# A rewritten end of a fused top-k attention and mixture-of-depths kernel, with its checks, half masks and gate transfers changed

## The chip, the cores and the metric

The kernel runs on one core of a Trainium2 chip. The metric is the device time of one execution in microseconds; the median of several runs is compared. The engines are named as in the profile: PE is the matrix engine (PEld its weight loads), DVE is VectorE, ACT is ScalarE, POOL is GpSimd, SP issues transfers.

## The reference

There are 8 batches, 8 heads, 576 tokens and a head dimension of 64. The first half is attention that keeps, for every query, the 32 highest scores:

```python
scores = scale * np.matmul(q, k.transpose(0, 1, 3, 2))
kth = np.partition(scores, -top_k, axis=-1)[..., -top_k:-top_k + 1]
scores = np.where(scores >= kth, scores, -1000000000.0)
attn = np.exp(scores - np.max(scores, axis=-1, keepdims=True))
attn = attn / (np.sum(attn, axis=-1, keepdims=True) + 1e-09)
x = np.matmul(attn, v)              # heads side by side: (8, 576, 512)
```

The second half is a mixture of depths: in each batch the 128 tokens with the highest gate score pass a two-layer network (512 to 1024 to 512), and the others are copied:

```python
scores = np.einsum('bsd,d->bs', x, w_gate)
top_idx = np.argpartition(-scores[b], 128)[:128]
ye = np.maximum(x[b, top_idx] @ w1, 0.0) @ w2
g = 1.0 / (1.0 + np.exp(-scores[b, top_idx]))
out[b, top_idx] = x[b, top_idx] + g[:, None] * ye
```

## The kernel before

**Units.** The 576 tokens of a batch are five tiles `t`: four of 128 tokens and one of 64 (`J` is 4, `NT` is 5, `R` is 64, `JP` is 512). A unit is one tile with two heads (for the last tile, two pairs of heads), 18 units a batch and 144 in all. The main loop (line 1210) goes over `n` and works on several units at a time: scores of unit n+1, the bound of n, what lies below the bound of n-1, the 32nd score of n-2, the mask of n-3, and weights times values of n-4.

**One unit.** PE multiplies queries and keys; ACT copies the scores to the tile `sc`. DVE takes the eight highest of seven parts (`cand`), and from these a bound (`bound`). ACT marks with a sign which scores lie above it (`sides`, with a count in `seen`), POOL multiplies (`y`), and DVE takes the eight highest of the rest (`next`); the last of them is the 32nd score. The mask `less` of a unit has two halves, one a head; `mask` (line 558) gives the first to ACT and the second to POOL, but in the units of `scatter_steps`, six in the loop, the second goes to DVE as a plain comparison. PE transposes scores and adds the mask times a large negative number, ACT takes the exponential (`pT`, `last`), and PE multiplies with the values (`av`); ACT copies to `xs`, and the sum of weights to `sums`. `normalise` takes a reciprocal on DVE and divides on POOL into `x`; `gates` (line 1070) makes the product with the gate weights on DVE (`prod`, `gate`).

**The mixture** of batch b (`mixture`, line 715) runs a step at a time between the units of batch b+1. Its gates go to DRAM (`row_dram`) and come back as one row in all partitions (`gate_row`). DVE counts how many gates are higher than each token's (`junk`, with the count in `rank`), a comparison with `slot` makes the selection matrix `pick`, and PE multiplies it with `parts` (place and gate, split into pieces by POOL in `split`) to find the rows. POOL fetches them by an indirect transfer (`xe`), PE runs the network (`h_ps`, `hT`, `y_ps`), and POOL adds the result to the output by another. The order is written out by hand: every engine wrapper `InOrder` (line 45) keeps program order, so all instructions show line 45, and lists such as `late` and `vector_late` say where a step is issued. `mix_at` gives the units of the steps; batch B-2, the last mixture in the loop, has earlier ones.

**Checks.** The fast way needs some conditions, or the general code in the `tc.If` at the end runs. `keep_least` (line 1189) takes per batch, on DVE, the least bound, the least 32nd score, and the least of a bit pattern (`low`). At the end `sure` collects all checks, and `unsure` is loaded into registers.

**The end.** After the loop four units of the last batch remain. `weigh_unit`, `values_unit` and `keep_unit` alternate between two sets of PSUM banks, the second taken from the scores' tile (`other_room`). The generator `closing` (line 862) does the last mixture: `spread` transposes the gates of four tiles and later of the last into `gate_row`, `count` counts (over 512 columns, then over 64 into `others`), three picks go to POOL and two to DVE, and the network follows with one product of 512 columns, one scaling `gy` and one indirect store. The remaining steps of the mixture of batch B-2 (`between`) lie in it.

Of the kernel before, what the change touches and what calls it, by code (L numbers as in the profile page):

```python
# [10 lines left out]
AF = mybir.ActivationFunctionType  # L11
# [37 lines left out]
def kernel(  # L49
# [45 lines left out]
    first_steps = ExitStack()  # L95
# [43 lines left out]
    least = const.tile([P, 3, B], FP32, name="least")  # L139
# [15 lines left out]
    others = const.tile([P, J], FP32, name="others")  # L155
# [28 lines left out]


# [372 lines left out]
    def mask(sc, next8, on=None):  # L558
# [5 lines left out]
        for i, engine in enumerate(on or (act, pool)):  # L564
            kth = next8[:, i, 7:8]
            if engine is act:
                act.activation(less[:, i, :], sc[:, i, :], AF.Relu, bias=kth, scale=-1.0)
            else:

                def is_less(engine=engine, i=i, kth=kth):  # L570
                    (engine or dve).tensor_scalar(
                        out=less[:, i, :],
                        in0=sc[:, i, :],
                        scalar1=kth,
                        scalar2=None,
                        op0=ALU.is_lt,
                    )

                if engine:
                    is_less()  # L580
                else:
                    vector_late.insert(0, is_less)
# [95 lines left out]
    def break_ties(t, gate, gate_row, rank):  # L678
# [14 lines left out]
        tok = stats.tile([P, 2], FP32, name="tok")  # L693
# [21 lines left out]
    def mixture(row0, pg, rank, exact=False):  # L715
# [20 lines left out]
        else:  # L736
            row_dram = drampool.tile([1, S], FP32, name="row_dram")
            sp.dma_start(
                out=row_dram[0, 0:JP].rearrange("(p j) -> p j", j=J), in_=gate[:, 0:J]
            )  # L740
            sp.dma_start(
                out=row_dram[0, JP:S].rearrange("(p j) -> p j", j=1),
                in_=gate[0:R, J:NT],
# [5 lines left out]
        for t in range(NT):  # L749
# [3 lines left out]
            def choose(t=t, n=n):  # L753
# [13 lines left out]
                if t == 0:  # L767
                    choose_slot(dve, t, n)
                else:
                    pool_late.append(lambda: choose_slot(pool, t, n))  # L770

            def choose_slot(engine, t, n):
                engine.tensor_scalar(
# [21 lines left out]
        found = stats.tile([P, 6], FP32, name="found")  # L795
        place = stats.tile([P, 2], FP32, name="place")
# [65 lines left out]
    def closing(b, pg, between):  # L862

        gate, rank = pg[0], ranks[:, b, :]
        gate_row = modpool.tile([P, S], FP32, name="gate_row")
        pick = modpool.tile([P, NT, CAP], BF16, name="pick")  # L870

        def spread(t0, t1):
            tr = ps_tr.tile([P, 2, J, P], FP32, name="ptr")
            n = R if t0 == J else P
            for t in range(t0, t1):
                pe.transpose(
                    tr[:, 0, t - t0, 0:n],
                    gate[0:n, t : t + 1].to_broadcast([n, P]),
                    ident[0:n, 0:n],
                )  # L880
            act.copy(
                out=gate_row[:, t0 * P : (t1 - 1) * P + n].rearrange(
                    "p (t i) -> p t i", i=n
                ),
                in_=tr[:, 0, 0 : t1 - t0, 0:n],
            )

        def count(t, among, rank):
            n = R if t == J else P
            junk = modpool.tile([P, S], FP32, name="junk", tag="scratch")  # L890
            dve.tensor_scalar(
                out=junk[0:n, among],
                in0=gate_row[0:n, among],
                scalar1=gate[0:n, t : t + 1],
                scalar2=None,
                op0=ALU.is_gt,
                op1=ALU.add,
                accum_out=rank[0:n, t : t + 1],
            )

        spread(0, J)
        yield
        for t in range(J):
            count(t, slice(0, JP), rank)
            if t == 1:
                yield
        yield
        spread(J, NT)
        split(*pg)
        for _ in range(2):  # L910
            next(between)
        for t in range(J):
            count(t, slice(JP, S), others)
        for t in range(J):
            (pool if t < 3 else dve).tensor_scalar(
                out=pick[:, t, :],
                in0=slot,
                scalar1=rank[:, t : t + 1],
                scalar2=others[:, t : t + 1],
                op0=ALU.subtract,  # L920
                op1=ALU.is_equal,
            )
        count(J, slice(0, S), rank)
        dve.tensor_scalar(
            out=pick[0:R, J, :],
            in0=slot[0:R, :],
            scalar1=rank[0:R, J:NT],
            scalar2=None,
            op0=ALU.is_equal,
        )  # L930
        ps = ps_av.tile([P, 512], FP32, name="av")[:, 0:6]
        place = stats.tile([P, 2], FP32, name="place")
        row_i = modpool.tile([P, 1], I32, name="row_i", bufs=2)
        g = modpool.tile([P, 1], FP32, name="g", bufs=2)
        multiply_places(ps, pick, pg)
        add_parts(place, ps)
        keep_rows(place, row_i, float(b * S), float((b + 1) * S - 1))
        xe = modpool.tile([P, HD], FP32, name="xe")
        fetch_rows(xe, out[0 : b + 1], row_i)
        dve.tensor_scalar_max(out=g, in0=place[:, 1:2], scalar1=-88.0)  # L940
        act.activation(g, g, AF.Exp, scale=-1.0)
        for _ in between:
            pass
        flush()
        flush_pool()
        yield
        dve.tensor_scalar_add(out=g, in0=g, scalar1=1.0)
        dve.reciprocal(out=g, in_=g)

        xeT = modpool.tile([P, NDC, CAP], FP32, name="xeT")  # L950
        ps = ps_tr.tile([P, 2, J, P], FP32, name="ptr")[:, 0, :, :]
        for dc in range(NDC):
            pe.transpose(ps[:, dc, :], xe[:, dc * P : (dc + 1) * P], ident)
        act.copy(out=xeT, in_=ps)
        yield
        hT = modpool.tile([P, NFC, CAP], FP32, name="hT")
        for f0 in range(0, NFC, 2):
            h_ps = (
                lambda: room_for_scores()[:, 0, 0, :],
                lambda: ps_av.tile([P, 512], FP32, name="av"),  # L960
                lambda: ps_misc.tile([P, 512], FP32, name="h_ps", tag="misc"),
                lambda: ps_tr.tile([P, 2, J, P], FP32, name="ptr")[:, 0, :, :].rearrange(
                    "p c i -> p (c i)"
                ),
            )[f0 // 2 % 4]()
            for i in range(2):
                multiply_h(h_ps[:, i * CAP : (i + 1) * CAP], f0 + i, xeT)
            act.activation(
                hT[:, f0 : f0 + 2, :],
                h_ps[:, 0 : 2 * CAP].rearrange("p (f i) -> p f i", f=2),  # L970
                AF.Relu,
            )
        ps = room_for_scores()[:, 0, 0, :]
        for fc in range(NFC):
            pe.matmul(
                ps, hT[:, fc, :], w2[:, fc, :], start=(fc == 0), stop=(fc == NFC - 1)
            )

        gy = modpool.tile([P, HD], FP32, name="gy")
# [563 lines left out]
```

## Time and profile before

| | us |
| --- | --- |
| median of 3 runs | 822.26 (820.8 to 823.27) |
| the profiled execution | 821.91 |
| its span, first to last instruction | 819.7 |
| VectorE busy | 782.5 |
| PE busy | 776.4 |
| ScalarE busy | 732.2 |
| GpSimd busy | 713.3 |

A busy PE is not PE at its peak, since matmuls are pipelined and their ends modelled; spans on POOL are rough. In rows of groups, the number after the bar is the busy time in us and then the mean of one in ns; the idle time before them follows, with what ended most of it. In timeline rows the first number is the start, the second the length, both in us; in brackets stands the idle time before.

### The profile page before, as it was taken

The numbers are of one execution on the slowest core, as the hardware profiler recorded it, in microseconds if no ns is written. First come the engines' busy times: TensorE is split into PE (matmuls) and PEld (weight loads), VectorE is DVE, ScalarE is ACT, GpSimd is POOL, SyncE is SP. The second block draws the span as 40 slices with busy tenths as digits, with TensorE's granted clock in tenths as the row PEclk, the third lists the DMA queues.
The fourth block names the chain that finished last, engine by engine and source line by source line (L and its number), as shares of the span: only waits on it lengthen the run. The fifth ranks groups of instructions, "written<-read, shape, count | busy, mean of one in ns | idle before, by whom it ended". The sixth has DMA issues, their size and how long they took to land. (4 is left out here: it accounts for less than half of the span.)

```text
span 819.7 us, 28408 instructions
## 1 busy us (share of the span) xinstructions
PE 776.4 (95%) x10215; PEld 597.1 (73%) x10215; DVE 782.5 (95%) x4650; ACT 732.2 (89%) x1567; POOL 713.3 (87%) x722
## 2 busy tenths in 40 slices
PE   8998888888999999999999999999999999999976
PEld 6766666666887777877787778877788777767744
DVE  7999999999999999999999999999999999999960
ACT  6999999999999999999999999999999999879830
POOL 4899999999999999899999999999989999899831
PEclk9999999999999999999999999999999999999999
DMA  7941115121151131422242221511305102101021
GB/s 163 296 84 40 41 53 100 34 53 29 60 112 41 28 92 24 104 47 43 64 83 52 53 40 60 112 34 35 74 27 113 28 15 66 23 14 16 2 72 30
DMA packets 122164, 50.38 MB, mean 61 GB/s; under 512 B 116448, under 2 KB 116448, under 8 KB 120992
## 3 DMA queue, kind: packets, MB, share of 16 engines
q1 hardware_dynamic: 118816, 43.94, 22.0%
q0 software_dynamic: 1728, 4.20, 2.8%
q8 instruction: 82, 1.34, 0.8%
q14 instruction: 66, 0.54, 0.3%
q10 hardware_dynamic: 1472, 0.36, 0.2%
HBM read 36.93 MB, written 11.55 MB: 59 GB/s over the span
## 5 line engine op out<-in xcount | busy, mean ns | idle before, releaser
L45 POOL TENSOR_TENSOR y<-sc,sides 128x576 f32<-128x576 f32 x288 | 365.7, 1291 | 52.4 <-ACT sides L45 49.3
L45 DVE MAX8 cand<-sc 128x8 f32<-128x82 f32 (+1 forms) x2016 | 314.0, 227 | 2.7 <-ACT sc L45 2.6
L45 POOL TENSOR_SCALAR less<-sc,next 128x576 bf16<-128x576 f32 x135 | 233.0, 1726 | 13.3 <-DVE next L45 9.7
L45 ACT ACTIVATE sides<-sc,bound 128x576 bf16<-128x576 f32 x288 | 223.0, 787 | 0.0
L45 PE MATMUL ptr<-out_of_reach,less 128*128 128x128 bf16 x1136 | 204.3, 219 | 18.5 <-POOL less L45 18.1
L45 PE MATMUL ptr<-ident,sc 128*128 128x128 f32 x1136 | 215.7, 281 | 0.0
L45 DVE MAX8 next<-y 128x8 f32<-128x584 f32 x288 | 204.4, 751 | 1.4 <-POOL y L45 1.4
L45 PEld LDWEIGHTS av<-v,pT 128*64 128x64 f32 x4544 | 144.1, 137 | 67.7 <-ACT last L45 64.7
L45 PEld LDWEIGHTS ptr<-ident,sc 128*128 128x128 f32 x1136 | 160.7, 141 | 28.1 <-issue 16.7
L45 ACT ACTIVATE pT<-ptr 128x1024 f32<-128x1024 f32 x142 | 145.3, 1023 | 32.1 <-PE ptr L45 30.1
L45 PE MATMUL ps<-kT,qT 64*128 64x288 f32 (+1 forms) x1248 | 173.9, 425 | 0.0
L45 PE MATMUL av<-v,pT 128*64 128x65 f32 x4544 | 163.7, 224 | 10.1 <-ACT last L45 9.2
L45 PEld LDWEIGHTS <-less 128*128 128x128 bf16 x1296 | 135.7, 105 | 38.0 <-POOL less L45 24.0
L45 ACT COPY sc<-ps 128x1152 f32<-128x1152 f32 x140 | 158.3, 1131 | 0.0
L45 ACT ACTIVATE less<-sc,next 128x576 bf16<-128x576 f32 x143 | 111.2, 778 | 13.2 <-DVE next L45 11.6
L45 PEld LDWEIGHTS ps<-kT,qT 64*128 64x128 f32 (+1 forms) x1248 | 95.8, 175 | 34.5 <-issue 20.8
L45 DVE MATCH_REPLACE8 cand<-best,cand 128x21 f32<-128x21 f32 (+1 forms) x576 | 98.9, 180 | 0.0
L45 DVE MAX8 best<-cand 128x8 f32<-128x21 f32 (+1 forms) x576 | 90.3, 189 | 0.0
L45 PE MATMUL h_ps<-xeT,w 128*128 128x128 f32 x464 | 65.8, 286 | 0.0
L45 PEld LDWEIGHTS h_ps<-xeT,w 128*128 128x128 f32 x464 | 55.8, 191 | 9.2 <-issue 5.8
L45 PE MATMUL y_ps<-w,hT 128*128 128x512 f32 x112 | 60.6, 636 | 0.0
L45 ACT ACTIVATION_READ_ACCUMULATOR sides<-sc,bound 128x1 f32 x288 | 60.0, 208 | 0.0
(157 smaller groups left out, 889.5 us busy)
## 6 DMA issues: line engine op xcount, KB each, us to landing
v<-in_v_dram SPq DMA_DIRECT2D x64, 128.0 KB, 3.5
out_dram<-x SPq DMA_DIRECT2D x8, 1024.0 KB
rows<-in_k_dram SPq DMA_DIRECT2D x56, 128.0 KB, 3.0
rows<-in_q_dram SPq DMA_DIRECT2D x56, 128.0 KB, 3.1
w<-in_moe_w_dram SPq DMA_DIRECT2D x2, 2048.0 KB
gate_row<-row_dram SPq DMA_DIRECT2D x7, 288.0 KB, 4.3
last<-in_q_dram SPq DMA_DIRECT2D x8, 128.0 KB
vpair<-in_v_dram SPq DMA_DIRECT2D x16, 64.0 KB, 3.9
```

Source lines behind the costliest of these rows:

```text
L45: return lambda *a, **kw: self._tc.keep_in_program_order(fn(*a, **kw))
```

## The change

In the loop:
- The check of the bounds' bits leaves `keep_least`: ACT copies each batch's bounds into a tile `bounded`, and `low` and two reductions are done once, at the end.
- DVE's half mask and the first slot of `pick` become a comparison whose results are also added up (`compare`); the sum of the mask is not used.
- The gates go to DRAM as 64 pieces of 16 bytes and 64 of 20, before as 128 of 16 and 64 of 4. The order in the row changes, which the counts don't depend on.

At the end:
- `closing` is gone, its steps stand in line. The last units use PSUM banks of their own (`ps_end`), and all their half masks are `compare` on DVE (`mask_both`).
- The gates of three tiles are spread and counted early, then the fourth's, then the last tile's. The last tile is divided on DVE. The picks are two on POOL, one on ACT in three steps, two on DVE.
- The fetched rows are transposed into two banks and copied by ACT and DVE. The checks follow, and their product on PE comes after the first layer. The second layer's product, the scaling and the store are done in two halves of 256 columns; `unsure` is loaded before the stores.

```diff
+    def compare(out, in0, scalar, op, total=None):
+        if total is None:
+            total = stats.tile([P, 1], FP32, name="some")[0 : out.shape[0], :]
+        dve.tensor_scalar(
+            out=out, in0=in0, scalar1=scalar, scalar2=None,
+            op0=op, op1=ALU.add, accum_out=total,
+        )
...
                 def is_less(engine=engine, i=i, kth=kth):
-                    (engine or dve).tensor_scalar(
+                    if engine is None:
+                        compare(less[:, i, :], sc[:, i, :], kth, ALU.is_lt)
+                        return
+                    engine.tensor_scalar(
...
             sp.dma_start(
-                out=row_dram[0, 0:JP].rearrange("(p j) -> p j", j=J), in_=gate[:, 0:J]
+                out=row_dram[0, R * NT : S].rearrange("(p j) -> p j", j=J),
+                in_=gate[R:P, 0:J],
             )
             sp.dma_start(
-                out=row_dram[0, JP:S].rearrange("(p j) -> p j", j=1),
-                in_=gate[0:R, J:NT],
+                out=row_dram[0, 0 : R * NT].rearrange("(p j) -> p j", j=NT),
+                in_=gate[0:R, 0:NT],
             )
...
                 if t == 0:
-                    choose_slot(dve, t, n)
+                    compare(pick[:, t, :], slot, rank[:, t : t + 1], ALU.is_equal)
...
     def keep_least(b, bound, kth):
-        low = stats.tile([P, per_batch, 2], I32, name="low", bufs=1)
-        dve.tensor_scalar(out=low, ...)
-        for w, of in enumerate((bound, kth, low)):
-            dve.tensor_reduce(out=least[:, w, b : b + 1], in_=of, ...)
+        at = 2 * per_batch * b
+        late.append(
+            lambda: act.copy(
+                out=bounded[:, at : at + 2 * per_batch].rearrange("p (n i) -> p n i", i=2),
+                in_=bound,
+            )
+        )
+        dve.tensor_reduce(out=least[:, b : b + 1], in_=kth, ...)
...
+    what_is_below(N - 1)
     weigh_unit(N - 4)
+    rows_ps = bank(ps_end, "av3")
+    turn_gates(0, J - 1, rows_ps)
     weighed[N - 4][2]()
-    what_is_below(N - 1)
-    mask_of(N - 3, (dve, dve))
+    keep_gates(0, J - 1, rows_ps)
+    mask_both(N - 3)
...
     weigh_unit(N - 1)
+    for t in range(2):
+        count(t, slice(0, (J - 1) * P), rank)
     gates(B - 1, J - 1)
+    count(2, slice(0, (J - 1) * P), rank)
...
+    count(J - 1, slice(0, JP), rank)
+    rden = stats.tile([P, H], FP32, name="rden")
+    dve.reciprocal(out=rden[0:R, :], in_=sums[0:R, (B - 1) * NT + J, :])
+    dve.tensor_tensor(x[0:R, J, :], xs[0:R, :, 0:D], rden[0:R, :], ALU.mult)
     store_last(last_out, x)
     gates(B - 1, J)
+    turn_gates(J, NT, tr)
+    keep_gates(J, NT, tr)
...
+    split(*pg)
+    count(J, slice(0, JP), rank)
+    for t in range(J - 1):
+        count(t, slice((J - 1) * P, S), others)
+    count(J - 1, slice(JP, S), others)
+    count(J, slice(JP, S), others)
+    for t in (0, 1):
+        pool.tensor_scalar(out=pick[:, t, :], in0=slot, ...)
+    act.activation(whole, others[:, 2:3], AF.Identity, bias=rank[:, 2:3])
+    act.activation(far, slot, AF.Abs, bias=whole, scale=-1.0)
+    act.activation(pick[:, 2, :], far, AF.Relu, bias=1.0, scale=-1.0)
+    for t in (J - 1, J):
+        dve.tensor_scalar(out=pick[0:n, t, :], in0=slot[0:n, :], ...)
...
+    for copy, half, dc in zip((act.copy, dve.tensor_copy), halves, (0, 2)):
+        copy(out=xeT[:, dc : dc + 2, :], in_=half[:, 0 : 2 * CAP])
...
+    for i in range(2):
+        for fc in range(NFC):
+            pe.matmul(halves[i][:, 0:W], hT[:, fc, :], w2[:, fc, i * W : (i + 1) * W], ...)
+    is_unsure = nc.values_load(unsure[0:1, 0:1])
+    for i in range(2):
+        dve.scalar_tensor_tensor(out=gy, in0=halves[i][:, 0:W], scalar=g[:, 0:1], ...)
+        put_rows(gy, half_i[:, i : i + 1], half_rows)
```

## The prediction

> **What bounds the kernel now.** I read the page's busy rows first, then the stages, then VectorE's waits, then the groups by shape.
>
> ```profile
> PE 776.4 (95%) x10215; PEld 597.1 (73%) x10215; DVE 782.5 (95%) x4650; ACT 732.2 (89%) x1567; POOL 713.3 (87%) x722
> ```
>
> Four engines are near full, so the shares do not name the bound. The windows by stage do (columns: stage, its length, then the busy time of PE, PEld, DVE, ACT, POOL, each with its instructions, then PE clock, DMA share, GB/s):
>
> ```profile
> 298.50:395.00 96.50, 95.02 (x1261) 73.57 (x1261) 96.39 (x577) 91.55 (x197) 88.60 (x88) 1.00 0.26 60
> 395.00:491.80 96.80, 95.04 (x1261) 73.60 (x1261) 96.14 (x578) 91.81 (x198) 88.85 (x88) 1.00 0.27 59
> 772.90:794.70 21.80, 17.23 (x230) 12.27 (x228) 14.22 (x41) 10.57 (x26) 9.94 (x16) 1.00 0.15 55
> 794.70:819.70 25.00, 17.98 (x93) 11.56 (x91) 4.70 (x26) 2.82 (x7) 3.70 (x3) 0.96 0.17 35
> ```
>
> In the loop (one batch is some 96.5 us) VectorE idles 0.1 to 0.7 us per batch: there its time is the kernel's time. From 772.9 us on nobody is full: the last 47 us are a chain of single steps. The waits of VectorE between 100 and 772 us confirm the first half, with one real stall:
>
> ```profile
> DVE junk L45 <- DMA gate_row<-row_dram: 1.8, 1, 1.8
> DVE cand L45 <- DVE best L45: 0.5, 1, 0.5
> ```
>
> So I cost the loop on VectorE alone and the end step by step. The groups of VectorE by shape give prices:
>
> ```profile
> L45 DVE CUSTOM_DVE_ANT_0 prod<-x,wg 128x512 f32<-128x512 f32 x32 | 30.3, 947 | 1.5 <-POOL x L45 1.4
> L45 DVE TENSOR_SCALAR_CACHE_REDUCE junk<-gate_row,gate 128x576 f32<-128x576 f32 x28 | 22.1, 788 | 1.9 <-DMA gate_row<-row_dram 1.8
> L45 DVE TENSOR_SCALAR low<-bound 128x36 int32<-128x36 int32 x8 | 6.9, 857 | 0.0
> L45 DVE TENSOR_SCALAR less<-sc,next 128x576 bf16<-128x576 f32 x10 | 6.6, 672 | 0.2
> ```
>
> The odd one is `low`: 36 numbers cost 857 ns on average. Its view gives 173 ns at least, 1,062 at the median; the timeline shows one at 395.09 for 1.06 us, while POOL's pair of `y` products ran from 393.58 to 396.06.
>
> **The loop, part by part.**
>
> *Bits checked at the end.* Per batch, `keep_least` loses `low` and two of three reductions. From the start of `low` to the next `cand` the timelines give 0.45, 1.52, 1.34, 1.34, 1.34, 1.33 and 1.29 us for seven batches: 8.6 in all. What stays is one reduction, about 0.13 from start to start: 0.9. So -7.7 us on VectorE. ScalarE gets a 36-wide copy per batch; the nearest row is its 128x8 `sums`, 0.22 us. I take nothing for it, because its own waits in the loop (17.6 us for `ptr` between 202 and 684 us) take it in; with that cover gone it is 7 x 0.2 = 1.4. Below nothing it cannot go, since it only adds work.
>
> Here a rule is weighed. The Trainium skill, "SBUF — State Buffer", on the shared port pair: VectorE in a two-port mode and GpSimd exclude each other for a whole instruction. That explains `low` at 1.06 against 0.17. It would also have every two-port mask blocked by POOL, so that the comparison with a sum, which I take to be out of that mode, pays. The rows say otherwise in the loop:
>
> *The half mask.* Six of the ten `less` lie in the loop, each in the unit in which POOL issues the scatter, and take 501 to 508 ns; the next instruction starts 0.42 us after (386.20 to 386.62). The four in the end take 1.52, 0.51, 1.15 and 0.52, two of them blocked. The comparison with a sum is the form of `junk`: 576 wide 788 ns, 0.80 to 0.86 from start to start with its accumulator read. So in the loop +0.41 x 6 = +2.5 us. By the rule alone, each blocked like the 1.15 row, it would be about -0.2 x 6 = -1.2. I take the rows.
>
> *The first slot.* Seven `pick` of 128 take 0.29 to 0.69 us, 1.9 us from start to start in all. With a sum, 128 wide lies between the 64-wide `junk` (0.32 apart) and the 512-wide (0.79): 0.39 x 7 = 2.7. So +0.8 us.
>
> *Gates to DRAM.* The issues and their landings:
>
> ```profile
> row_dram<-gate SPq DMA_DIRECT2D x7, 2.0 KB, 2.4
> row_dram<-gate SPq DMA_DIRECT2D x7, 0.2 KB, 7.2
> ```
>
> The first is 128 pieces of 16 bytes, the second 64 of 4 bytes, three times as long from issue to landing. SP waits 41.1 us in six batches for them; the gate row goes out only then (issued 710.37, landed after 4.3). Only batch 6, whose mixture starts early, shows it on VectorE, the 1.8 us above. "DMA: Bandwidth & Descriptors", Specifications, has every transfer under 512 B do read-modify-write; by that 20 and 16 bytes are as bad as 4, and the gain is nothing. The rows separate 16 from 4 sharply. Pieces of 20 are no row, but nearer to 16: I take a landing of 2.4 to 4 us. The stall needs 1.85 less than 7.2 to vanish, so it vanishes: -1.85; kept end 0. In the other six batches the row lands before it is asked for (131.49 + 4.3 against 139.2), so nothing. The loads queued behind on SP go out earlier, with room anyway.
>
> Loop: -7.7 + 2.5 + 0.8 - 1.85 = -6.25. PE is close behind (its weight loads wait 41.1 us for ScalarE's `last` in the five batches from 202 to 684, some 0.5 a unit, in heavy mixture units nothing), and POOL with a `divide` needs 5.5 us a unit; I let 0.5 be given back: -5.75.
>
> **The end, step by step** (clock of the profile before; DVE steps from start to start).
>
> ```profile
> 779.59 0.77 ACT L45 ACTIVATE less<-sc,next 128x576 bf16<-128x576 f32 x1 [0.95 <-DVE next L45]
> 780.33 0.52 DVE L45 TENSOR_SCALAR less<-sc,next 128x576 bf16<-128x576 f32 x1
> 781.66 0.33 PE L45 MATMUL ps<-ident,sc 128*128 128x128 f32 x1 [1.32 <-ACT xs L45]
> 787.75 1.04 POOL L45 TENSOR_TENSOR x<-xs,rden 64x512 f32<-64x512 f32 x1 [4.54 <-DVE rden L45]
> 791.25 2.40 POOL L45 TENSOR_SCALAR pick<-slot,ranks,others 128x128 bf16<-128x128 f32 x3
> 798.31 0.63 PE L45 MATMUL ptr<-ident,xe 128*128 128x128 f32 x4 [0.66 <-DMA xe<-out_dram,row_i]
> 806.86 7.03 PE L45 MATMUL ps<-w,hT 128*128 128x512 f32 x16
> 814.01 0.75 DVE L45 SCALAR_TENSOR_TENSOR gy<-ps,g,xe 128x512 f32<-128x512 f32 x1 [14.77 <-PEq L1506]
> 815.04 1.01 POOL L45 DMA_INDIRECT out_dram<-gy,row_i  x1 [14.44 <-DVEq L1506]
> ```
>
> - Masks: all six halves on VectorE, 6 x 0.86 + 3 x 1.33 for `next` from 771.51: done at 780.7. Before, with two on ScalarE but two blocked, 780.85. Even. `sides` of the last unit go ahead of an exponential, so POOL's `y`, 778.76 before, is there at about 777 and not waited for.
> - The last transposes: before, PE waited until 781.66 for the bank that `xs` was copied from. Separate banks leave only the mask: they end at 781.75 instead of 783.3. Values and copies follow; `sums` at 785.5 instead of 787.45.
> - VectorE no longer has four 512-wide counts before the last tile (three tiles' columns are spread early and counted 384 wide). Divide on VectorE, 64x512, the length of the 0.69 `prod`, instead of POOL's 1.04: gate of the last tile ready at 787.35 instead of 789.9, -2.55.
> - Counts of the rest: 192 wide 0.45 x 3, 64 wide 0.32 x 2, behind the 0.78 count of the last tile that covers PE's and ScalarE's turn: done 790.2. Picks: two on POOL (0.61 to 0.80 each, behind `split`, done 790.2), one on ScalarE in three steps of about 0.3 (790.4), two on VectorE (790.95). PE is through at 791.2 instead of 794.0: -2.8.
> - Place, row, fetch, landing unchanged, 4.2 us: rows at 795.4. The 3.7 us of y products in between still fit (791.2 to 794.9).
> - Transposes and copy in halves on ScalarE and VectorE: 1.15 instead of 1.37 from landing to first product: -0.2. The checks (now 288 wide, about 5 us) run on VectorE under the 7.2 us of h products; their one product costs PE 0.15.
> - Output in two halves: the second scaling is 128x256, 0.45 instead of 0.75: -0.3. Both halves take PE 3.5 us each, the same 7.03.
>
> Together -2.8 - 0.2 + 0.15 - 0.3 = -3.15; a smaller last transfer may give 0.2 more. I take -3.3.
>
> **Sum.** -5.75 - 3.3 = -9.05 against 821.91 of the profiled execution (span 819.7, 2.2 around it), which lies 0.35 under the median of the runs, 822.26. Against the median: 813.2.
>
> **Rivals.**
> 1. *Pieces of 20 bytes land as late as those of 4.* For it: only 16 is measured fast; against: 4-byte pieces are four times as many to each 16. The 1.85 stays: 815.1. Chance 0.21.
> 2. *The loop gives back.* PE, ScalarE or POOL, all at 92 to 98% of a batch, end the unit in which `low` was taken out; half of the 4.4 (the loop without the stall) returns, 2.2 instead of my 0.5: 814.9. For it: PE's waits are nothing in some mixture units; against: 0.5 a unit elsewhere, and five score tiles of depth. Chance 0.17.
> 3. *The second half's scatter waits.* It is ordered behind the landing of the first, since both write the output: first issued about 808.0, landed 3.1 later as the last one does now, 811.1; the second is ready at 811.5. Only 0.4 of room; if the first takes 5.0 like the accumulating scatters, +1.5: 814.7. Chance 0.05.
> 4. *Slower: the dot products meet POOL.* `prod` takes 0.67 free, 1.94 at worst, 947 ns at the mean of 32. The shift of VectorE against POOL can raise that. All is lost when the mean of 40 rises by 9.05 / 40 = 0.23, to 1.18 us; slower by over 0.3% beyond 1.24: 825. Against: POOL's order hangs on VectorE's results each unit, so phases come back. Chance 0.09, of which 0.05 ends within 0.3% of before.
>
> That the change does not take effect is no case: the order of instructions has every step.
>
> **Numbers.** Main case 0.48: 813.2, its own range 811 to 815 (collisions of `prod`, up to 12 us in all now, may also fall). Rivals 1 to 3 end at 814.7 to 815.1, 1 and 2 together at 816.8, with part of 3 at 817.5. Below, a third of the collisions gone: 809. About 0.3% (2.5 us) is what a measurement here tells from no change. Faster 0.91, same 0.05, slower 0.04.
>
> **What would show it.** Right: no `low` in the loop; `junk` without a DMA wait; both `row_dram` issues near 2.4 to 4 us; loop `less` at 0.79; the last batch's fetch about 2.8 us nearer to the end of the loop; from landing of rows to end some 20.9 instead of 21.4. Wrong: `prod` above 1.1, new waits of `cand` or `next` on ScalarE or POOL in the loop, a POOL wait ahead of the last scatter.

## The result, and the profile after

The changed kernel takes 817.04 us (815.27 to 817.24, six runs) where the kernel before took 821.72 beside it: a ratio of 0.9936, with an interval of 0.9921 to 0.995. It is faster by 4.7 us, about half of the 9.05 forecast. It lies outside the main case's own range of 811 to 815 us and within the 809 to 817.5 us over which the prediction spread all its cases.

The page's busy row:

```profile
PE 777.2 (95%) x10231; PEld 600.3 (74%) x10231; DVE 784.2 (96%) x4655; ACT 730.3 (90%) x1577; POOL 721.8 (89%) x722
```

Four engines are still near full, and VectorE is as busy as before although work was taken from it. In the profiled execution (817.24, span 815.4) a first load landed later, so that the first `next` starts at 20.86 us instead of 18.96. The change has no part in that; a later run of the same kernel starts at 18.81, and two of the six executions here took 815.3 and 815.4 us. Loops are therefore compared below from their own first `next`.

The windows by stage, two batches of the loop and the two parts of the end, in the columns of the prediction (busy time of PE, PEld, DVE, ACT, POOL, then PE clock, DMA share, GB/s):

```profile
303.71:399.64 95.93, 94.87 (x1264) 73.42 (x1262) 95.78 (x576) 91.15 (x198) 90.48 (x88) 1.00 0.26 60
399.64:495.57 95.93, 94.86 (x1264) 73.40 (x1263) 95.79 (x576) 91.18 (x198) 90.50 (x88) 1.00 0.26 60
770.40:791.20 20.80, 18.95 (x245) 13.87 (x244) 17.34 (x55) 11.32 (x30) 9.47 (x15) 1.00 0.15 58
791.20:815.40 24.20, 17.77 (x108) 14.48 (x106) 5.86 (x27) 2.75 (x7) 4.18 (x4) 0.93 0.17 37
```

A batch now takes 95.93 us instead of 96.5 to 96.8, the end 45.0 us from the `next` of unit 141 on instead of 48.15.

The groups that answer to those of before (busy us, then the mean in ns):

```profile
L45 DVE CUSTOM_DVE_ANT_0 prod<-x,wg 128x512 f32<-128x512 f32 x32 | 34.6, 1082 | 0.4 <-POOL x L45 0.3
L45 DVE TENSOR_SCALAR_CACHE_REDUCE less<-sc,next 128x576 bf16<-128x576 f32 x12 | 9.3, 797 | 0.0
L45 DVE TENSOR_SCALAR_CACHE_REDUCE junk<-gate_row,gate 128x576 f32<-128x576 f32 x28 | 22.1, 788 | 0.0
```

`junk` has no wait for a DMA any more, `less` costs 797 ns, and `prod` has become 135 ns longer at the mean. The issues of the gates land in 2.0 us (16-byte pieces) and 1.6 us (20-byte pieces), where the 4-byte pieces took 7.2:

```profile
row_dram<-gate SPq DMA_DIRECT2D x7, 1.0 KB, 2.0
row_dram<-gate SPq DMA_DIRECT2D x7, 1.2 KB, 1.6
```

Unit by unit the loop shows two things. At `keep_least` VectorE gains 1.02 to 1.25 us in six batches and 0.2 in the first, 6.8 in all. In the very next unit it loses 0.19 to 0.78 again, 4.0 in all, because the `prod` there has become longer. The timeline at one of these places, first of before, then of after (start, length):

```profile
398.95 2.53 POOL L45 TENSOR_TENSOR y<-sc,sides 128x576 f32<-128x576 f32 x2
401.62 1.73 POOL L45 TENSOR_SCALAR less<-sc,next 128x576 bf16<-128x576 f32 x1
402.26 0.67 DVE L45 CUSTOM_DVE_ANT_0 prod<-x,wg 128x512 f32<-128x512 f32 x1
```

```profile
400.37 2.53 POOL L45 TENSOR_TENSOR y<-sc,sides 128x576 f32<-128x576 f32 x2
402.00 1.45 DVE L45 CUSTOM_DVE_ANT_0 prod<-x,wg 128x512 f32<-128x512 f32 x1
402.86 0.67 POOL L45 TENSOR_TENSOR y<-steps,seen 128x16 f32<-128x16 f32 x1
```

Before, `prod` came 0.8 us after POOL's two passes of `y`; now it comes into the second pass, waits for its end at about 402.9, and then holds up POOL's next step in turn. The trace books the wait as VectorE's busy time, so no view of waits shows it. This is what the prediction's fourth rival described. The experiments ask whether it is the cause of the loss or only its form.

The end stands nearly as it was forecast:

```profile
785.28 0.68 DVE L45 CUSTOM_DVE_ANT_0 prod<-x,wg 64x512 f32<-64x512 f32 x1
787.41 1.58 POOL L45 TENSOR_SCALAR pick<-slot,ranks,others 128x128 bf16<-128x128 f32 x2
788.78 0.59 DVE L45 TENSOR_SCALAR pick<-slot,ranks,others 128x128 bf16<-128x128 f32 x2
789.74 0.31 PE L45 MATMUL av<-parts,pick 128*128 128x6 bf16 x3 [0.51 <-ACT pick L45]
794.31 0.66 PE L45 MATMUL av<-ident,xe 128*128 128x128 f32 x4 [0.63 <-DMA xe<-out_dram,row_i]
802.55 0.19 PE L45 MATMUL av<-ones,sure 128*1 128x1 f32 x2
810.64 0.96 POOL L45 DMA_INDIRECT out_dram<-gy,half_i  x1 [2.44 <-POOLq L1578]
```

The last tile's gate, the picks and the places come one after the other without a long wait; ScalarE's `pick` is the last of the five; the check's product runs behind the first layer; the last store waits for nothing but its branch.

### The profile page after: what moved, and what is told of

It reads as the page before. It is cut to its first block, busy times and chain, and to the rows that moved or that the text cites. A ratio compares the mean times of both kernels' runs of the same rounds, so it can differ in the third digit from the quotient of the medians.

```text
span 815.4 us, 28453 instructions
## 1 busy us (share of the span) xinstructions
PE 777.2 (95%) x10231; PEld 600.3 (74%) x10231; DVE 784.2 (96%) x4655; ACT 730.3 (90%) x1577; POOL 721.8 (89%) x722
## 5 line engine op out<-in xcount | busy, mean ns | idle before, releaser
L45 PEld LDWEIGHTS av<-v,pT 128*64 128x64 f32 x4608 | 146.1, 137 | 66.1 <-ACT last L45 62.8
L45 PE MATMUL av<-v,pT 128*64 128x65 f32 x4608 | 166.0, 224 | 8.3 <-ACT last L45 7.6
```

The costliest lines, as they stand in the source:

```text
L45: return lambda *a, **kw: self._tc.keep_in_program_order(fn(*a, **kw))
```

## The experiments

Ratios are to the kernel before, which ran beside each kernel.

### The parts alone

Four kernels are the kernel before with one part of the change. The first moves the bits to the end and leaves the old end in place (some small tiles have fewer buffers, for room):

```diff
-        low = stats.tile([P, per_batch, 2], I32, name="low", bufs=1)
-        dve.tensor_scalar(out=low, in0=bound.bitcast(I32), ...)
-        for w, of in enumerate((bound, kth, low)):
-            dve.tensor_reduce(out=least[:, w, b : b + 1], in_=of, ...)
+        late.append(lambda: act.copy(out=bounded[...], in_=bound))
+        dve.tensor_reduce(out=least[:, b : b + 1], in_=kth, ...)
...
+    flush()
+    low = modpool.tile([P, S], I32, name="low", tag="scratch")[:, 0:NS]
+    dve.tensor_scalar(out=low, in0=bounded.bitcast(I32), ...)
```

> The kernel before with only the bounds' bits moved to the end (low and two reductions leave keep_least; a copy on ScalarE; the end as before, but for 288-wide checks). Theory A (the dot product of the next unit meets GpSimd and gives it back): in batches 2 to 6 the unit of keep_least is 1.0 to 1.25 us shorter, the prod that follows takes about 1.4 us instead of 0.67, and the net is 0.3 us a batch: 2 to 3 us below before. Theory B (VectorE's saving is kept unless another engine ends the unit): prod stays at 0.67, 1.1 us a batch kept, 6.5 to 7.5 us below before.

It took 824.94 us (ratio 1.0049, interval 1.0032 to 1.0066): slower. Its loop is shorter by 2.6 us up to unit 141, which is what theory A summed up to, but not by its working: the `prod` behind `keep_least` took 1.02 to 1.05 us in five of the batches instead of 1.4, and the rest was lost at the plain masks and picks, which now waited (the masks took 1.22 us at the median). From the last unit's `next` to the end it takes 47.45 us instead of 40.87. Its timeline there:

```profile
798.00 0.31 DVE L45 TENSOR_SCALAR low<-bounded 128x288 int32<-128x288 int32 x1 [3.96 <-ACT bounded L45]
802.71 0.19 PE L45 MATMUL av<-ones,sure 128*1 128x1 f32 x2 [4.43 <-DVE g L45]
802.83 3.78 PE L45 MATMUL ps<-xeT,w 128*128 128x128 f32 x16
806.40 3.21 PE L45 MATMUL av<-xeT,w 128*128 128x128 f32 x16
```

The last copy of the bounds stands behind `gy` on ScalarE, VectorE's checks start after it and take 4.7 us, and PE has their product ahead of the first layer. Then the first layer's products take 3.78 and 3.21 us, at a granted clock of 0.50 and 0.59; in the changed kernel they take 2.05 and 1.95 at 1.00.

The second sends the gates in pieces of 16 and 20 bytes:

```diff
-                out=row_dram[0, 0:JP].rearrange("(p j) -> p j", j=J), in_=gate[:, 0:J]
+                out=row_dram[0, R * NT : S].rearrange("(p j) -> p j", j=J),
+                in_=gate[R:P, 0:J],
...
-                out=row_dram[0, JP:S].rearrange("(p j) -> p j", j=1),
-                in_=gate[0:R, J:NT],
+                out=row_dram[0, 0 : R * NT].rearrange("(p j) -> p j", j=NT),
+                in_=gate[0:R, 0:NT],
```

> The kernel before with only the gates' pieces of 16 and 20 bytes. Theory A and B alike: both transfers land after about 2 us, the one wait of the counts for the gate row (1.8 us, batch 6) is gone, and units before and after keep their lengths: 1.8 us below before. If other engines were near their bound in that unit, part of it returns: under 1 us.

819.85 us, ratio 0.9991 (0.9983 to 0.9999). The stall of the gate row is gone (1.95 us earlier in that unit), and 0.77 of it returns six units later, where a `prod` goes from 0.67 to 1.44 us.

The third writes VectorE's masks and the first slot as comparisons with a sum (here too some small tiles have fewer buffers):

```diff
-                    (engine or dve).tensor_scalar(
+                    if engine is None:
+                        compare(less[:, i, :], sc[:, i, :], kth, ALU.is_lt)
+                        return
+                    engine.tensor_scalar(
...
-                    choose_slot(dve, t, n)
+                    compare(pick[:, t, :], slot, rank[:, t : t + 1], ALU.is_equal)
```

> The kernel before with only VectorE's half mask and the first slot in the loop as comparisons with a sum (the end's masks stay plain). Theory A (a plain comparison is shorter and was not blocked in these six units): less 0.50 to 0.79 us, 0.3 us longer in each of six units and up to 0.2 in seven for the slot where it was not blocked: 1.5 to 2.5 us above before. Theory C (the plain form holds GpSimd up by as much): no change within 0.5 us, or below.

821.52 us, ratio 1.0013 (1.0002 to 1.0023): each of the six masks costs 0.3 us more (0.72 from its start to that of the next instruction, before 0.42).

The fourth has the new end, with the old loop (`closing` gone, its steps in line as in the diff of the change).

> The kernel before with only the end rewritten (checks of the bits per batch as before, plain half mask, slot and pieces in the loop as before). From the trace of the changed kernel, the end is 3.2 us shorter counted from the last unit's first steps; that should stand alone: 3.0 to 3.5 us below before. If the end gained only because the loop left the engines in another phase: under 2 us. The four parts together, if they add: the difference of the changed kernel to before, plus or minus 1 us.

817.22 us, ratio 0.9954 (0.9938 to 0.9969): 3.1 us faster, as the end was costed.

The four differences are +4.7, -0.4, +1.2 and -3.1 us, +2.4 together, while the change as a whole gives -4.9 in the repeat below. So the parts act on each other. One candidate is the end: the bits there may only pay with the check's product behind the first layer. Without the 6.6 us by which the first kernel's end was longer, the four would come to -4.2.

### The masks, the phase and the place of `prod`

The next four start from the changed kernel. First the changed kernel again:

> The changed kernel as it is, on the chip of the other three, to compare them with: 817.0 us (815 to 817.5), and in each batch but the first one dot product `prod` of about 1.45 us where the trace of before has 0.67.

815.85 us, ratio 0.9945 (0.9933 to 0.9957). `prod` has the same lengths as in the first trace of it, 0.78, 0.86, 0.97, 1.46 and 0.96 us for the five of the fifth batch.

Then the plain comparisons in the loop again:

```diff
-                    if engine is None:
-                        compare(less[:, i, :], sc[:, i, :], kth, ALU.is_lt)
-                        return
-                    engine.tensor_scalar(
+                    (engine or dve).tensor_scalar(
...
-                    compare(pick[:, t, :], slot, rank[:, t : t + 1], ALU.is_equal)
+                    dve.tensor_scalar(out=pick[0:n, t, :], in0=slot[0:n, :], ...)
```

> The changed kernel with VectorE's half masks and the first slot in the loop written as plain comparisons again (the end keeps its sums). A plain comparison of 576 numbers took 0.50 us on VectorE in the trace of before, the one with a sum 0.79. If the plain form only costs its own time, six masks become shorter by 0.3 us and the kernel is 1.8 us faster than the changed one. If the plain form waits for POOL's `y` once the loop runs earlier, as ten of them did when the bits alone were moved (median 1.22 us there), each becomes longer by 0.4 us or so, and the kernel is 2 us or more slower.

815.64 us, ratio 0.9945 (0.9932 to 0.9957): no difference, which neither expectation had. The groups say why:

```profile
L45 DVE TENSOR_SCALAR less<-sc,next 128x576 bf16<-128x576 f32 x6 | 6.6, 1097 | 0.0
L45 DVE CUSTOM_DVE_ANT_0 prod<-x,wg 128x512 f32<-128x512 f32 x32 | 29.2, 913 | 0.4 <-POOL x L45 0.3
```

The plain masks do wait now (1,097 ns at the mean; five of the six about 1.21 us, one 0.50). But `prod` becomes shorter: all forty take 37.6 us instead of 43.7 in the repeat. What is waited at one place isn't waited at the next.

The filler at `keep_least`:

```diff
-        dve.tensor_reduce(out=least[:, b : b + 1], in_=kth, ...)
+        for _ in range(4):
+            dve.tensor_reduce(out=least[:, b : b + 1], in_=kth, ...)
+        if b < B - 1:
+            spare = stats.tile([P, 8], FP32, name="spare", bufs=1)
+            dve.max(out=spare, in_=scs[per_batch * (b + 1) - 1][:, 0, :])
```

> The changed kernel with a filler at keep_least that does nothing for the result: three more small reductions of the same 36 numbers and one MAX8 over 576 scores, together about 1.07 us of VectorE's time in each batch, about what the change took away there; none of it is of a form that waits for POOL in the traces. Theory 1: what the change gained at keep_least was taken back because VectorE now reaches `prod` in the unit after it while POOL is still in `y`. Then the filler restores the old phase, `prod` there is 0.67 us again instead of 1.45, and the kernel is slower by only 0.3 us a batch, 2 us in all (819). Theory 2: VectorE's time simply adds up and the loss of 4 us lies elsewhere: then slower by 7 to 8.5 us (824 to 825.5). Theory 3: another engine ends the unit, and the filler costs nothing (817).

819.79 us, ratio 0.9988 (0.9979 to 0.9997). The filler is larger than I had worked out: 1.42 us at each place. In the next unit 0.76 to 1.06 of it comes back in the later batches, and the fourth `prod` of a batch is 0.67 to 0.68 us again. Up to the last unit 3.8 us remain of about 10. So the first theory's mechanism is there, at twice the 2 us that it put; the second, a plain sum, falls, and so does the third, no cost. From the third batch on a batch takes 96.73 to 96.75 us, and here VectorE's share is the largest:

```profile
401.56:498.30 96.74, 94.94 (x1265) 73.40 (x1261) 96.50 (x581) 91.79 (x198) 88.59 (x88) 1.00 0.25 59
```

`prod` ahead of the first head's maxima:

```diff
-            vector_late.append(lambda a=gating: gates(*a))
...
+        if gating is not None:
+            gates(*gating)
         if is_unit(n):
             bound_of(n)
```

> The changed kernel with one thing moved: the dot product `prod` and the read of its sum stand ahead of the seven `cand` maxima of the unit's first head instead of behind them, about 1.0 us earlier on VectorE. In the trace of the changed kernel a `prod` that starts while POOL is in a pass of `y` takes what is left of that pass and 0.55 us: 0.24 left gave 0.79, 0.42 gave 0.97, 0.88 gave 1.43. At the new place 0.01 to 0.24 us of a pass are left for four of the five in a batch and 0.66 for the fifth. Theory 1 (the wait for POOL's pass is what VectorE pays): 0.2 us less for each of some 35, so 3 to 7 us faster than the changed kernel (810 to 814), less where POOL's second pass, now held up by 0.55 us, comes late for somebody. Theory 3 (another engine ends the unit): no difference.

821.51 us, ratio 1.0006 (0.9998 to 1.0013), 5.7 us slower than the changed kernel beside it. Both expectations fall. The group shows that the waits grew:

```profile
L45 DVE CUSTOM_DVE_ANT_0 prod<-x,wg 128x512 f32<-128x512 f32 x32 | 36.8, 1151 | 1.4 <-POOL x L45 1.3
```

I had worked out new waits from the phase of an old trace. But the phase moved along: the five of a batch (the fifth) met 0.2 to 1.2 us of a pass in the new trace, and took 0.78, 1.24, 0.98, 1.73 and 1.04 us.

### A later place, and the port taken out

`prod` behind the maxima of both heads:

```diff
-            vector_late.append(lambda a=gating: gates(*a))
+            after_cand.append(lambda a=gating: gates(*a))
...
+        while after_cand:
+            after_cand.pop(0)()
         parts = cand.rearrange("p i (u e) -> p i u e", u=PARTS)
```

> The changed kernel with the dot product `prod` and the read of its sum moved behind the `cand` maxima of both heads, about 1.07 us later on VectorE than now. In the trace of before, a `prod` that starts after the second pass of `y` ends 1.44 us after that pass at the earliest and takes 0.67 us where it is the later; from the changed kernel's trace the five of a batch would then start 0.82, 0.75, 0.65, 0.17 and 0.65 us behind the pass and take 0.67, 0.69, 0.79, 1.27 and 0.79 us, 4.2 us together instead of 5.0. If VectorE pays each wait in full, and POOL is not disturbed because it isn't in `y`: 0.8 us a batch, 4 to 6.5 us faster than the changed kernel (809.5 to 812). If what VectorE saves at one place it waits at the next for POOL's port, so that the two engines hold each other's pace: within 1.5 us of the changed kernel.

813.77 us (813.45 to 814.21), ratio 0.9912 (0.9899 to 0.9926): faster than both kernels, the interval wholly below that of the changed kernel's repeat. At 2.1 us below that repeat it meets neither of the two ranges. The gain stops early:

```profile
300.41:395.45 95.04, 93.97 (x1255) 72.57 (x1253) 94.90 (x576) 90.28 (x195) 89.53 (x87) 1.00 0.26 61
395.45:491.38 95.93, 94.86 (x1264) 73.41 (x1263) 95.79 (x577) 91.17 (x198) 90.52 (x88) 1.00 0.26 60
```

Up to 395 us its batches are shorter than the changed kernel's but for one; from there on a batch takes the same 95.9 us, and the five `prod` again take 0.76, 0.86, 0.96, 1.43 and 0.96 us, though they stand at another place in the order.

So far the later batches end at 95.9 us or above, whether `prod` is slowed or quickened. The next two kernels ask for the floor under it. `prod` is replaced by the sum of `x` alone, in the form with a sum; the gate's weights are left out:

```diff
-        dve.tensor_tensor_reduce(
-            out=prod[0:n, 0:HD], in0=x, in1=wg[0:n, :],
-            scale=1.0, scalar=0.0, op0=ALU.mult, op1=ALU.add, accum_out=g,
-        )
+        dve.tensor_scalar(
+            out=prod[0:n, 0:HD], in0=x, scalar1=1.0, scalar2=None,
+            op0=ALU.mult, op1=ALU.add, accum_out=g,
+        )
```

> The kernel before with each dot product replaced by the sum of `x` alone in one pass (TENSOR_SCALAR_CACHE_REDUCE with 512 numbers; the gate's weights are left out, so the gates have other values): by the row of 788 ns for 576 numbers, 0.71 us or so, a form that didn't wait for POOL in any trace. The 40 dot products took 39.0 us there, so 10 us less VectorE time in it; the end has five of them. Serves as the base of the next run. If VectorE pays waits in full: 9 to 11 us faster than before; if it waits elsewhere instead: 0 to 5.

> The changed kernel with the same replacement (the gate's weights left out). Nothing of VectorE's in the loop is then of a form that waited for POOL, the 40 products' 43.7 us become 28 to 30. Theory 1 (the change's gain in the loop was eaten by `prod` waiting for POOL's `y`): the gain of the change comes out in full, this run is 8 to 10 us faster than the run with the same replacement in the kernel before, instead of 4.9. Theory 3 (the other engines set the loop's pace, and VectorE would wait for one of them): the difference stays at 5 us or falls, and VectorE shows new waits in the loop, for POOL's `y` or ACT's `sc`.

With these gates both kernels go on into the general code behind the `tc.If` (4,365 and 4,362 us), so their totals say nothing and only the loops are read. From the first `next` to that of the eighth batch the two take 662.6 and 660.3 us; with `prod` it was 669.8 and 666.9 (the latter in the repeat). The change is worth 2.3 us here and 2.9 there. The first theory's 8 to 10 us fall; the third's pace set by another engine stands. The windows of the changed kernel without `prod`:

```profile
203.96:298.30 94.34, 93.23 (x1247) 71.86 (x1246) 94.10 (x576) 89.61 (x195) 86.68 (x87) 1.00 0.27 61
393.64:489.55 95.91, 94.81 (x1269) 73.37 (x1267) 94.81 (x576) 91.16 (x199) 88.29 (x88) 1.00 0.27 60
489.55:585.48 95.93, 94.81 (x1268) 73.39 (x1265) 94.79 (x575) 91.15 (x199) 88.25 (x88) 1.00 0.25 60
```

At first VectorE runs ahead. Then a batch takes 95.9 us again, with VectorE's busy time down to 94.8, a microsecond below the length of the batch. PE's column hasn't moved: 94.81 here, 94.87 in the changed kernel.

### PE, and the check's product

The last kernel adds a small product on PE in each unit, and in the end puts the check's product ahead of the first layer:

```diff
             tr, av = room_to_turn()
+            pe.matmul(tr[:, 0, 0, :], out_of_reach, out_of_reach)
...
+    ps = bank(ps_av, "av")
+    pe.matmul(ps[0:1, 0:1], sure, ones)
+    dve.tensor_scalar(out=unsure, in0=ps[0:1, 0:1], ...)
     hT = modpool.tile([P, NFC, CAP], FP32, name="hT")
...
-    ps = bank(ps_av, "av")
-    pe.matmul(ps[0:1, 0:1], sure, ones)
-    dve.tensor_scalar(out=unsure, in0=ps[0:1, 0:1], ...)
```

> Two edits to the changed kernel that lie in different stretches of it, so that the trace tells them apart. In the loop: one more 128x128 bf16 matmul in each unit (into a tile that is overwritten at once; a row of twenty such in the trace took 1.29 us, so 65 ns each, 1.2 us in a batch of 18 units). If PE sets the pace of the later batches (95.9 us each in the changed kernel from the third on), they become longer by the whole 1.2 us or a little more, and the last unit's `next` comes 5 to 9 us later. If VectorE sets it, PE has the time to spare and nothing moves by more than 1 us. In the end: the matmul of the check (`ones`, `sure`) and the copy of its result stand ahead of the first layer again, as in the kernel before. From the last unit's `next` to the end of the span the changed kernel takes 39.4 us. If the bits at the end only pay because that matmul was moved behind the first layer, PE waits for VectorE's checks ahead of it, and the stretch takes 5 to 7 us more; if VectorE's checks would be ready anyway, less than 1 us more. Total by the first pair of theories and this: 827 to 832.

827.82 us, ratio 1.0094 (1.008 to 1.0107). The loop, two of its windows:

```profile
206.26:302.47 96.21, 95.07 (x1273) 73.33 (x1271) 95.98 (x576) 90.41 (x198) 89.69 (x87) 1.00 0.25 60
399.45:496.53 97.08, 96.03 (x1284) 74.12 (x1282) 96.94 (x576) 91.27 (x198) 90.57 (x88) 1.00 0.24 59
```

The later batches take 96.98 to 97.08 us, longer by 1.0 to 1.2 with one exception (0.8, against a 96.19 of the repeat), and PE's busy time rises by 0.8 to 1.3. The last unit's `next` comes 5.6 us later. ScalarE's 91.3 and POOL's 90.6 of 97.08 us leave room. So PE, with its own waits, sets the pace there: 94.8 us of work and about 1.0 us a batch in which its values wait for ScalarE's `last`. The row is from three batches of the repeat (total, times, longest):

```profile
PE av L45 <- ACT last L45: 3.1, 6, 0.8
```

VectorE's column rises along (96.94) although VectorE was given nothing: what it shows beyond its work is waiting for POOL inside `prod`, whose sum goes from 43.7 to 47.9 us.

In the end, from the last `next` on, it takes 46.5 us instead of 39.4: 7.1 more. PE's waits have the row, and the windows around it the clock:

```profile
PE av L45 <- DVE ones L45: 5.1, 1, 5.1
```

```profile
799.00:804.20 5.20, 0.09 (x2) 0.03 (x2) 4.71 (x23) 0.41 (x2) 1.62 (x1) 0.89 0.39 50
804.30:807.80 3.50, 3.50 (x18) 3.50 (x17) 0.14 (x1) 0.00 (x0) 0.00 (x0) 0.50 0.01 2
807.90:810.60 2.70, 2.70 (x17) 2.70 (x17) 0.00 (x0) 0.38 (x1) 0.00 (x0) 0.63 0.00 0
```

PE waits 5.1 us for VectorE's checks, and after that its granted clock is 0.50 and then 0.63 at the mean, so that the products behind it are slow as well. In the first experiment the same wait was 4.43 us and the clock behind it 0.50, and its end was longer by 6.6 us: this is what made it slower.

The lengths of the batches on VectorE, from the first `next` of one to that of the following, in us (worked out from the timelines):

| kernel | 2nd | 3rd | 4th | 5th | 6th | 7th |
| --- | --- | --- | --- | --- | --- | --- |
| before | 97.15 | 96.09 | 96.54 | 96.68 | 96.13 | 96.06 |
| changed | 96.12 | 95.48 | 95.93 | 95.93 | 95.94 | 95.91 |
| changed, filler on VectorE | 96.17 | 96.74 | 96.73 | 96.74 | 96.74 | 96.75 |
| changed, `prod` behind both heads | 95.34 | 95.63 | 95.04 | 95.93 | 95.95 | 95.90 |
| before, sum instead of `prod` | 94.06 | 95.87 | 95.88 | 95.87 | 96.01 | 95.82 |
| changed, sum instead of `prod` | 93.62 | 94.34 | 95.34 | 95.91 | 95.93 | 95.85 |
| changed, product added on PE | 96.11 | 96.21 | 96.98 | 97.08 | 96.99 | 97.01 |

The same on PE, from its first transposition of scores into `av` in one batch to that in the following. The last three columns say how far that transposition lies behind the `next` of the same unit, at the start of a batch:

| kernel | PE's 3rd | 4th | 5th | 6th | behind `next`, 3rd | 4th | 5th |
| --- | --- | --- | --- | --- | --- | --- | --- |
| before | 96.10 | 96.54 | 96.67 | 96.13 | 4.44 | 4.45 | 4.44 |
| changed | 95.90 | 95.95 | 95.90 | 95.94 | 5.82 | 6.25 | 6.26 |
| changed, filler on VectorE | 96.45 | 96.73 | 96.73 | 96.74 | 4.40 | 4.10 | 4.10 |
| changed, `prod` behind both heads | 95.90 | 95.95 | 95.91 | 95.95 | 6.11 | 6.38 | 7.28 |
| changed, sum instead of `prod` | 95.90 | 95.95 | 95.91 | 95.94 | 5.99 | 7.55 | 8.16 |
| changed, product added on PE | 96.96 | 97.12 | 96.96 | 97.01 | 5.88 | 6.62 | 6.76 |

In the kernel before, and with the filler, PE keeps a near-fixed distance behind `next` and takes VectorE's lengths: there VectorE leads, as the prediction had it, and so the filler costs time. In the changed kernel PE takes 95.90 to 95.95 us from the third batch on, also with `prod` moved behind both heads or replaced, whatever VectorE does meanwhile. VectorE's shorter batches are a lead over PE: the distance grows as long as they last (from 5.99 to 8.16 us without `prod`) and then stands. With the product added, PE's own batches take 96.96 us and more from the third on.

## Why the prediction was right, and where its size was off

The direction and the end were forecast by the right mechanism. The loop's gain was not: it was costed at 5.75 us and came to 1.4 to 3.0, by the traces compared. The total stays within the spread of the cases because the end held and because the prediction had priced a loop that gives back.

**The end: right.** Forecast -3.3, measured -3.15 from unit 141's `next` on (45.0 us instead of 48.15), and -3.1 for the end alone. Counted from that `next`, the last tile's gate comes 2.9 us earlier (forecast 2.55), the places 2.9 (2.8), the rows at the forecast time. ScalarE's pick was the last, not VectorE's. That the checks run under the first layer was costed at 0.15; their place is worth 7.1 us, which the last experiment shows.

**Bits out of the loop: right at its place, given back after it.** `keep_least` lost 6.8 us (forecast 7.7). The step that failed is "I let 0.5 be given back". The loop up to unit 141 was to gain 5.75 and gained 3.0 in the first trace and 2.3 in the repeat, each from its own first `next`. (The run with the end alone keeps the old loop, and there it took 751.7 us where the trace of before has 752.55; against it the gain is 2.1 and 1.4.) The prices of the single steps were not at fault: where they act, -6.8 for the bits, +1.8 for the masks, nothing for the slot and -1.9 for the stall are -6.9, the forecast sum -6.25. The step rests on an earlier one, that in the loop VectorE's time is the kernel's time. That holds only down to PE's pace. The second to seventh batch took 578.65 us before; six times 95.9 are 575.4, so 3.2 us were to be had there by PE's pace (and a little more as a lead), and the changed kernel took 575.31. The row for it stood in the prediction: PE busy 95.02 of 96.50 us. What I read as slack were the waits of PE's weight loads for `last` (41.1 us in five batches); of the matmuls themselves, the view of waits of before has only this between 200 and 680 us, five batches:

```profile
PE av L45 <- ACT last L45: 5.6, 12, 0.8
```

That is 1.1 us a batch, and 95.0 and 1.1 leave 0.4 of 96.5.

**How VectorE loses what it gained.** By waiting inside `prod` for POOL (sum of the forty 39.0 before, 43.0 after). In the changed kernel's trace, `prod` takes what is left of the pass of `y` that it meets and 0.55 us: 0.24 left gave 0.79, 0.42 gave 0.97, 0.88 gave 1.43. This agrees with the Trainium skill, "SBUF — State Buffer", Who interferes with whom: an instruction of VectorE with two inputs in SBUF contends with a GpSimd instruction that reads there, and the one that comes second waits for the whole of the other. Beside POOL's mask `less` the trace does not bear out the whole: the `prod` of before at 402.26 takes its free 0.67 us although `less`, which reads `sc`, runs from 401.62 to 403.35 (spans on POOL are rough). The loss looks like that contention but isn't caused by it alone: with the contention out, the later batches take the same 95.9 us. That the first batches can run below 95.9 is VectorE's growing lead over PE, as the second table shows. How PE's pace then reaches VectorE (by ScalarE's `sc` and `sides` and POOL's `y`, I suppose) was argued and not traced.

**Masks with a sum: forecast +2.5, in the changed kernel nothing.** Alone they cost 0.3 us each (costed at 0.41). In the changed loop the plain form waits (1.21 us), as the rule says that the prediction put aside, and the total is the same either way. The free rows of before (0.50 us) held for before's phase only. **The slot**, forecast +0.8, costs nothing: 347 ns, before 362 with one blocked among them.

**Gates to DRAM: right.** 1.6 and 2.0 us to land, better than the 2.4 to 4 forecast, and the stall is gone (-1.88 in that unit). Rival 1 falls. Alone, the pieces bring 0.4 us (interval of the ratio 0.9983 to 0.9999), part of the stall being waited by a `prod` again.

**The other rivals.** Rival 2, the loop gives back because another engine ends the unit, is what happened, with PE as the engine, and it came out dearer than its price of 2.2: of the 6.25 summed up, 3.3 to 4.0 were given back (up to 4.8 against the loop of the run with the end alone). The total's nearness to 816.8, the end of rivals 1 and 2 together, is luck: rival 1 did not come. Rival 3 falls: the second store waited only for its branch. Rival 4 had the right instruction and a mean of 1.08 us instead of 0.947, far from the 1.18 from which it would have eaten all.

Sum in the repeat, by span against the profile of before: 2.3 from the loop, 3.15 from the end and 0.15 from the start are the 5.6 us between 819.7 and 814.1. Between the medians it is 4.9: the traced execution of before, at 821.91 us, lies above the 820.79 of the kernel before beside the repeat.

## What to carry to other kernels

Before costing an edit on the engine that looks fullest, add up for each of the others its work and the waits of its own stream in the same stretch: the gain ends where the next of them is full, here 0.5 us a batch below. An engine's busy time can hold waiting for a port; replace the suspected instruction by one that doesn't use the port, and look whether the length of the stretch changes. And don't work out the new place of an instruction from the phases of an old trace, since the phases move along: of the two places tried, one cost 5.7 us and one brought 2.

## What was not expected of the hardware

PE's granted clock fell to 0.50 after a wait of 5.1 us, and a group of sixteen products took 3.78 us instead of 2.05; after a wait of 4.43 us it was 3.78 again. The Trainium skill, "TensorE: Matmul & The Clock Gate", What's actually happening, has the clock at half after an idle window of some 3.4 us; waits of up to 1.5 us left the clock at 1.00 in the end of before (PE waits 1.53 us there ahead of the last tile's gates), and where the kernels stay out of the general code, no trace has a wait between that and 4.43. So 5.1 us of waiting made the end 7.1 us longer.

Pieces of 16 and 20 bytes to DRAM landed in 2.0 and 1.6 us, pieces of 4 bytes in 7.2, though they were 64 beside the 128 of 16 bytes before (2.4 us). Pieces of 16 and of 20 bytes are alike here; the 4-byte ones are dear. Why was not tested.
